# An attention and mixture kernel: every place in the order of issue chosen anew

## The chip, the core and the metric

The kernel runs on one NeuronCore of one Trainium2 chip. The core has engines that each work through a queue of their own, in the order in which the program issued to it: TensorE (matmuls, written PE in the profile, with its weight loads as PEld), VectorE (DVE), ScalarE (ACT), GpSimd (POOL) and SyncE (SP), which here issues all DMA transfers. Engines wait for one another through semaphores. SBUF is the working memory, PSUM the memory that matmuls write to, in banks of 128 partitions by 512 fp32 numbers.

The metric is the device time of one execution in microseconds (us).

## What is computed

The reference is attention with a mask, for 4 batches of 8 heads, 768 positions and 64 channels, followed by a soft mixture of 8 experts with 4 slots each. Cut to what matters:

```python
q_bits = (einsum('bhsd,dk->bhsk', q, proj) > 0)        # 6 bits per position
k_bits = (einsum('bhsd,dk->bhsk', k, proj) > 0)
mask = q_bucket[:, :, :, None] == k_bucket[:, :, None, :]   # all six bits agree
scores = where(mask, scale * q @ k.T, -1e9)
attn = exp(scores - scores.max(-1))
attn = attn / (attn.sum(-1) + 1e-9)
x = attn @ v                                   # then (batch*seq, heads*dim) = (3072, 512)

logits = x @ phi                               # 32 slots
d = softmax of logits over the 3072 rows
slot_input = d.T @ x
slot_out[e] = relu(slot_input[e] @ w1[e]) @ w2[e]
c = softmax of logits over the 32 slots
out = c @ slot_out
```

All inputs and the output are fp32.

## The kernel before

There are 32 heads (`BH`), each with six tiles of 128 positions (`NT`). Two heads form a pair, because two times 64 channels fill the 128 partitions; eight heads form a batch. The work of a head is cut into small functions, each of which issues a few instructions, often to several engines:

- `load(h)` brings q and k of a pair to the one tile `raw`. `split_hi` (ScalarE, L327) rounds them to the tile `w4`, `split_lo(h, x)` (L331, GpSimd for the first pair and VectorE for the others) takes the rest. `bits` (L365 on TensorE, L358 on VectorE) makes the bucket bits as rows. For head 0, `bits` writes the rows directly and `bits_copy` and `bits_rest` make those of head 1.
- `spread_y`, `spread_l`, `spread_x` and `spread_bits` (all L335) are DMA transfers from `w4` and the bit tile into the operands X and Y of the score matmuls; `spread_bits` is four transfers, `spread_x` two, the others one. There are three such operand tiles, used in turn. `load_v` brings v. `first_y` (POOL) fills constant rows once.
- `smax(h, t, part)` (L406) multiplies for the row maxima, into two PSUM buffers (`smx`); `most(h, n)` (L413, L416) takes the maxima on VectorE. Per head there are twelve of the one and nine of the other, since some parts share a bank. A third `smax` bank can only be written when the maximum of an earlier one has been taken.
- `shift(h)` (VectorE, L423 to L426) turns the maxima into the shift of the exponent, `shift_rows(h)` (L445, for head 0 L440) transposes it and sends it as a row into X.
- `scores(h, i, part)` (L460) multiplies the scores into three PSUM buffers (`st`), `exps(h, n)` (ScalarE, L466) takes the exponential to SBUF, again nine per head. `acc` (L474, L477) adds the exponentials on GpSimd for the row sums, and `av` (L486) multiplies them with v; the last `av` of a head ends in a copy on ScalarE (L490).
- Per pair follow `pair_sum` (L498, with a copy to the one buffer `sm`, L501), `pair_turn` (L533), `pair_rec` (three reciprocals, L505), `pair_log` (L513), `pair_add` (L525, L527) and `pair_x` (L548, L550). Per batch follow `batch_both`, `batch_max`, `batch_exp` (L660), `batch_turn` (L681, copy L683 into `sm`), `batch_scale`, `batch_slots` (L698), `batch_weigh`, `batch_share` and `batch_arrange`.
- At the end the `one_` functions do a head alone what the `pair_` functions do for two, `batch_spin` (L766, L767) transposes weights for the last product, and the experts' matmuls (L911, L962) and the output (L983) follow, which are not in the plan.

What sets the order is a plan written out as numbers. One place stands for a tile of a head, so a head has six places and a pair twelve. `at(when, f, ...)` gives each function call a place: `WHEN` holds places relative to the head's (or the pair's) first place and is used for all heads alike, once for even and once for odd heads where it has two lists; `FIRST` replaces single calls at the start and `LAST` at the end. The plan is sorted by place and issued in that order; each engine gets its queue from it. Between places the loop also frees memory pools and issues weight loads:

```python
    plan.sort(key=lambda w: w[:2])
    for slot in range(int(plan[0][0] // 1), last + 5):
...
        while plan and plan[0][0] < slot + 1:
            f, *args = plan.pop(0)[2]
            f(*args)
```

Since a place only sorts, two plans differ for an engine only where two calls that both issue to it change their order. In the plan before, each `most` has the place of its last `smax` plus 0.0005, and each `exps` that of its last `scores`, so that each follows its matmul directly.

Of the kernel before, what the change touches and what calls it, by code (L numbers as in the profile page):

```python
# [75 lines left out]

FIRST = {('load', 4): 4.476,
 ('bits', 2): 1.288,
 ('split_hi', 2): 0.833,
 ('split_lo', 2, 0): 1.029,  # L80
 ('split_lo', 2, 1): 2.366,
 ('spread_y', 2): 1.587,
 ('spread_bits', 2): 1.668,
 ('spread_l', 2): 2.667,
 ('spread_x', 2): 3.34,
 ('smax', 1, 0, 0): -1.746,
 ('smax', 1, 0, 1): -1.169,
 ('smax', 1, 1, 0): 0.452,
 ('smax', 1, 1, 1): 0.57,
 ('smax', 1, 2, 0): 1.478,  # L90
 ('smax', 1, 2, 1): 1.593,
 ('smax', 1, 3, 0): 2.035,
 ('smax', 1, 3, 1): 2.061,
 ('smax', 1, 4, 0): 2.241,
 ('smax', 1, 4, 1): 2.696,
 ('smax', 1, 5, 0): 2.774,
 ('smax', 1, 5, 1): 3.433,
 ('first_y', 1): -20.551,
 ('first_y', 2): -3.524,
 ('spread_y', 1): -14.012,  # L100
 ('spread_l', 0): -12.047,
 ('spread_bits', 1): -7.869,
 ('bits_rest',): -7.878,
 ('bits_copy',): -13.916,
 ('most', 1, 0): -1.7455,
 ('most', 1, 2): 0.4525,
 ('most', 1, 3): 0.5704999999999999,
 ('most', 1, 4): 1.4785,
 ('most', 1, 6): 2.0355000000000003,
 ('most', 1, 7): 2.0615,  # L110
 ('most', 1, 8): 2.2415000000000003,
 ('most', 1, 10): 2.7745,
 ('most', 1, 11): 3.4335}

LAST = {('one_sum', -1): 1.725,
 ('one_log', -1): 1.7251,
 ('one_turn', -1): 1.7252,
 ('one_x', -1): 1.7253,
 ('one_rec', -1): 1.7255,
 ('one_add', -1): 1.7256,  # L120
 ('one_put', -1): 3.7252,
 ('batch_max', -1): 3.7249,
 ('batch_exp', -1): 3.7253,
 ('batch_turn', -1): 3.7265,
 ('batch_scale', -1): 3.7275,
 ('batch_spin', -4, 0): 1.7254,
 ('batch_spin', -4, 1): 3.7251,
 ('batch_spin', -3, 0): 3.7252,
 ('batch_spin', -3, 1): 3.7254,
 ('batch_spin', -2, 0): 3.7256,  # L130
 ('batch_spin', -2, 1): 3.7266,
 ('one_sum', -2): -2.605,
 ('one_log', -2): -3.569,
 ('one_fold', -1): -2.008,
 ('one_turn', -2): -2.223,
 ('one_rec', -2): -1.562,
 ('one_add', -2): -1.292,
 ('one_x', -2): -0.77,
 ('one_put', -2): 0.78,
 ('acc', -1, 1): -2.422,  # L140
 ('acc', -1, 2): -2.051,
 ('acc', -1, 3): -2.05,
 ('acc', -1, 4): -0.27500000000000036,
 ('acc', -1, 5): -0.274,
 ('av', -1, 0): -2.487,
 ('av', -1, 1): -2.486,
 ('av', -1, 2): -0.9130000000000003,
 ('av', -1, 3): -0.9119999999999999,
 ('av', -1, 4): -0.13600000000000012,
 ('av', -1, 5): 0.7329999999999997}  # L150


def constants():
# [880 lines left out]
```

## Time and profile before

| | us |
|---|---|
| median of 3 runs (513.42 to 513.77) | 513.61 |
| the profiled execution | 512.31 |
| its span, from the first to the last instruction | 510.3 |

| engine | busy, share of the span | instructions |
|---|---|---|
| VectorE, row maxima L416 and L413 | 129.4 us and 65.2 us | 192 and 96 |
| ScalarE, exponentials L466 | 156.5 us | 288 |
| GpSimd, row sums L477 and L474 | 237.8 us and 58.4 us | 125 and 32 |
| TensorE, scores L460 | 175.3 us | 768 |
| TensorE, row maxima L406 | 121.6 us | 384 |
| TensorE, av L486 | 143.1 us | 768 |

The profiler's ends of matmuls are modelled and overlap, so the busy times of TensorE's lines are not what each costs; the distance between two landmarks of the same kind is. In rows of a timeline stand the start, the duration, the engine, the line, the operation, the tiles written and read, and the count of instructions merged into the row; in brackets the idle time before and who ended it. Rows of the chain in order of time have start, duration, engine, tile, line and count.

### The profile page before, as it was taken

The page shows a single profiled execution, that of the slowest core. Times are in us where ns is not written, and L with a number is a line of the kernel's source. Part 1 is how long each engine was busy: PE and PEld are TensorE (multiplying, and loading weights), DVE is VectorE, ACT ScalarE, POOL GpSimd, SP SyncE. Part 2 cuts the span into 40 slices and gives each one's busy share as a digit, 9 for nine tenths or more (in the row PEclk, how much of TensorE's full clock was granted, in tenths as well). Part 3 has the DMA queues.
Part 4 walks back from the last instruction along what each step waited for, and adds up shares of the span by engine and source line. Part 5 has one row for each costly group of instructions (what it writes and reads, how often), then busy time and mean ns, then how long its engine had stood idle before and what let it go on. Part 6 is the DMA issues. An engine that isn't in the chain of part 4 may idle for free.

```text
span 510.3 us, 8930 instructions
## 1 busy us (share of the span) xinstructions
PE 491.0 (96%) x3140; PEld 287.7 (56%) x3140; DVE 358.0 (70%) x674; ACT 242.3 (47%) x481; POOL 322.3 (63%) x200
## 2 busy tenths in 40 slices
PE   6999999999999999999999999999999999989992
PEld 4555656565655556565655565656555565544562
DVE  5685877777877788777778787878766875464133
ACT  4135545544545545454564545555455454542132
POOL 8037777768676977768587876776759786800000
PEclk9789999999999999999999999999999999999997
DMA  5765666657675767666766576766456276797987
GB/s 139 197 141 147 193 171 197 171 181 176 199 165 166 176 195 173 199 172 187 181 186 166 147 208 163 207 167 196 110 137 154 70 161 223 265 395 295 412 320 299
DMA packets 39728, 99.57 MB, mean 195 GB/s; under 512 B 7298, under 2 KB 13700, under 8 KB 39684
## 3 DMA queue, kind: packets, MB, share of 16 engines
q1 hardware_dynamic: 39684, 99.00, 67.2%
q8 instruction: 25, 0.41, 0.3%
q14 instruction: 19, 0.16, 0.1%
HBM read 52.76 MB, written 6.29 MB: 116 GB/s over the span
## 4 chain that ended last, share of the span: by engine, by line
PE 83%; DVE 9%; DMA 3%; ACT 2%; issue 1%; SPq 0%; DVEq 0%; ACTq 0%
PE st L460 24%; PE av L486 22%; PE smx L406 14%; DVE mx L416 3%; PE qs L962 3%; PE qh L911 3%; PE mi L365 2%; DVE mx L413 2%; PE mi L498 2%; PE mi L513 2%; PE mi L548 2%; PE mi L445 2%; DMA w<-w 1%; PE av L290 1%; PE mi L698 1%; DMA XY<-w 1%
## 5 line engine op out<-in xcount | busy, mean ns | idle before, releaser
L477 POOL TENSOR_TENSOR acc<-acc,pt 128x768 f32<-128x768 f32 x125 | 237.8, 1902 | 65.0 <-ACT pt L466 51.2
L466 ACT ACTIVATE pt<-st 128x512 f32<-128x512 f32 x288 | 156.5, 596 | 58.3 <-PE st L460 54.5
L460 PE MATMUL st<-XY 128*128 128x256 f32 (+1 forms) x768 | 175.3, 342 | 0.8 <-ACT pt L466 0.3
L416 DVE TENSOR_REDUCE mx<-smx 128x1 f32<-128x512 f32 x192 | 129.4, 681 | 48.7 <-PE smx L406 48.0
L486 PE MATMUL av<-pt,v 128*64 128x384 f32 x768 | 143.1, 500 | 0.0
L460 PEld LDWEIGHTS st<-XY 128*128 128x128 f32 x768 | 123.2, 190 | 19.6 <-ACT pt L466 5.1
L406 PE MATMUL smx<-XY 96*128 96x512 f32 (+1 forms) x384 | 121.6, 371 | 5.1 <-DVE mx L416 3.8
L406 PEld LDWEIGHTS smx<-XY 96*128 96x128 f32 x384 | 65.7, 191 | 54.5 <-issue 15.2
L486 PEld LDWEIGHTS av<-pt,v 128*64 128x64 f32 x768 | 48.2, 137 | 65.5 <-issue 55.4
L474 POOL TENSOR_TENSOR acc<-pt 128x768 f32<-128x768 f32 x32 | 58.4, 1825 | 34.9 <-ACT pt L466 34.7
L413 DVE TENSOR_REDUCE mx<-smx 128x2 f32<-128x512 f32 x96 | 65.2, 679 | 15.0 <-PE smx L406 14.4
L490 ACT COPY avs<-av 128x384 f32<-128x384 f32 x32 | 15.3, 477 | 61.1 <-PE av L486 61.1
L331 DVE TENSOR_TENSOR w<-raw,w 128x768 fp32r<-128x768 f32 x30 | 37.8, 1259 | 1.0 <-ACT w L327 1.0
L505 DVE RECIPROCAL sm<-sm 128x128 f32<-128x128 f32 x45 | 38.3, 907 | 0.0
L448 ACT CAST mr<-mi 12x128 fp32r<-12x128 f32 x31 | 7.9, 254 | 64.0 <-PE mi L445 53.3
L327 ACT CAST w<-raw 128x768 fp32r<-128x768 f32 x32 | 25.1, 831 | 12.6 <-DMA XY<-w 6.9
L358 DVE TENSOR_SCALAR bt<-mi,con 128x384 fp32r<-128x384 f32 x15 | 10.1, 676 | 18.2 <-PE mi L365 11.7
L550 DVE TENSOR_TENSOR xq<-mi,r 128x256 f32<-128x256 f32 x45 | 17.4, 414 | 2.1 <-PE mi L548 1.2
L445 PEld LDWEIGHTS mi<-ident,mz 128*72 128x72 f32 x31 | 3.5, 114 | 21.6 <-DVE mz L426 12.8
L365 PE MATMUL mi<-raw,pb 128*32 128x384 f32 x128 | 15.1, 517 | 0.1
L548 PE MATMUL mi<-ident,avs 128*128 128x128 f32 x90 | 14.8, 272 | 0.0
L962 PE MATMUL qs<-w 128*32 128x256 f32 x232 | 14.6, 380 | 0.0
(171 smaller groups left out, 318.0 us busy)
## 6 DMA issues: line engine op xcount, KB each, us to landing
w<-w SPq DMA_DIRECT2D x61, 512.0 KB
XY<-w SPq DMA_DIRECT2D x63, 384.0 KB
raw<-qk SPq DMA_DIRECT2D x32, 384.0 KB
XY<-w SPq DMA_DIRECT2D x64, 192.0 KB
v<-vt SPq DMA_DIRECT2D x32, 192.0 KB
out<-w SPq DMA_DIRECT2D x12, 512.0 KB
xq<-w SPq DMA_DIRECT2D x3, 512.0 KB
XY<-bt SPq DMA_DIRECT2D x62, 19.5 KB
```

What stands on the lines that cost most here:

```text
L331: (nc.vector if h else nc.gpsimd).tensor_tensor(out=w[:, 2 * x + 1], in0=st[h]["raw"][:, x], in1=w[:, 2 * x], op=ALU.subtract)
L365: nc.tensor.matmul(pts_b[j // 2 if h == 0 else 0][32 * j:32 * j + 32, 0:HC], pb[:, 32 * (j // 2):32 * (j // 2) + 32], st[h]["raw"][:, j // ...
L406: nc.tensor.matmul(pt[:, o:o + b - a], s["Y"][0:96, 0, t * P:(t + 1) * P], s["Y"][0:96, 1, a:b], start=True, stop=True)
L413: nc.vector.tensor_reduce(out=mx[:, n - 1:n + 1], in_=s["sm_ps", n - 1].rearrange("p (a x) -> p a x", a=2), axis=AX.X, op=ALU.max)
L416: nc.vector.reduce_max(out=mx[:, n:n + 1], in_=s["sm_ps", n], axis=AX.X)
L460: nc.tensor.matmul(pt[:, o:o + b - a], x[:, 1, i * P:(i + 1) * P], x[:, 0, a:b], start=first, stop=not first)
L466: nc.scalar.activation(s["P", n // 4][:, 512 * u:512 * u + 512], s["st_ps", n - (n % 4 == 2)], AF.Exp, scale=D ** -0.5)
L474: nc.gpsimd.tensor_tensor(out=s["acc"], in0=pr[:, 0:S], in1=pr[:, S:2 * S], op=ALU.add)
L477: eng.tensor_tensor(out=s["acc"], in0=s["acc"], in1=pr[:, a * S:(a + 1) * S], op=ALU.add)
L486: nc.tensor.matmul(s["av"][64 * c:64 * c + 64, 0:HC], s["v"][:, i, :], pr[:, o + c * HC:o + (c + 1) * HC], start=(i == 0), stop=(i == NT - 1))
L505: nc.vector.reciprocal(out=rs[:, k * P:(k + 1) * P], in_=rs[:, k * P:(k + 1) * P])
L962: nc.tensor.matmul(po[32 * j:32 * j + 32], hTs[g][:, f, 32 * j:32 * j + 32], wt[1, x, 2 * g + f // 4, j][:, (f % 4) * HM:(f % 4 + 1) * HM] ...
```

## The change

All numbers of `WHEN`, `FIRST` and `LAST` are replaced, and calls whose place lies after the end of the loop are issued after it. The places of `most` and `exps` are now free numbers: a maximum or an exponential can stand later in its engine's queue than directly behind its matmul. The two `av` of a tile pair, which stood 0.001 apart, have places of their own too. No function changes, so that every instruction is issued as before, in another order.

Cut to the parts with most of the calls:

```diff
-WHEN = {'load': -23.228,
- 'bits': -14.718,
- 'split_hi': -14.15,
- 'split_lo': [-13.173, -12.657],
- 'spread': [[-13.185, -11.633, -9.493, -7.304], [-10.44, -10.41, -11.057, -10.018]],
- 'load_v': [-3.955, -4.754],
...
- 'shift': [-2.803, -2.153],
- 'shift_rows': [-2.18, -2.143],
- 'av': [[3.488, 3.489, 6.789, 6.79, 7.032, 7.033], [3.202, 3.203, 4.62, 4.621, 6.466, 6.4670000000000005]],
- 'pair_sum': 15.98,
- 'pair_rec': [18.062, 18.408, 18.445],
- 'pair_log': 18.701,
- 'pair_add': 19.165,
- 'batch_exp': 22.194,
- 'batch_turn': 23.394,
- 'batch_slots': 24.562,
- 'load_weights': 4.18,
- 'most': [[-7.7205, -7.1035, -6.7585, -6.1825, -5.5425, -5.9395, -4.4195, -3.9885, -3.4575], [-7.8065, -7.7095, -7.1565, -7.0925, -4.5085, -5.3165, -2.7865, -3.8375, -5.7855]],
+WHEN = {'load': -22.0508,
+ 'bits': -14.467,
+ 'split_hi': -14.3621,
+ 'split_lo': [-13.3303, -12.2413],
+ 'spread': [[-11.312, -10.3184, -8.8177, -6.6655], [-12.6618, -9.5428, -9.5016, -10.4378]],
+ 'load_v': [-3.4958, -2.5158],
...
+ 'shift': [-2.9192, -2.4824],
+ 'shift_rows': [-2.406, -2.3767],
+ 'av': [[3.3475, 3.579, 6.7431, 6.9618, 7.1119, 7.1448], [3.0065, 3.033, 4.3979, 4.45, 6.3731, 6.7119]],
+ 'pair_sum': 15.6351,
+ 'pair_rec': [19.6428, 18.3203, 19.2569],
+ 'pair_log': 18.6723,
+ 'pair_add': 19.6831,
+ 'batch_exp': 21.1538,
+ 'batch_turn': 23.5591,
+ 'batch_slots': 27.233,
+ 'load_weights': 0.3156,
+ 'most': [[-8.0236, -7.5536, -7.3039, -6.8101, -3.9785, -5.9175, -3.4914, -3.5661, -3.1213], [-7.7877, -7.733, -6.7829, -6.5887, -3.7858, -4.368, -2.779, -2.8697, -5.5832]],
...
 FIRST = {
- ('bits', 2): 1.288,
- ('split_lo', 2, 0): 1.029,
- ('split_lo', 2, 1): 2.366,
- ('smax', 1, 1, 1): 0.57,
- ('smax', 1, 5, 0): 2.774,
- ('first_y', 1): -20.551,
- ('bits_rest',): -7.878,
- ('most', 1, 0): -1.7455,
- ('most', 1, 11): 3.4335}
+ ('bits', 2): -2.2897,
+ ('split_lo', 2, 0): 0.9772,
+ ('split_lo', 2, 1): 3.8714,
+ ('smax', 1, 1, 1): -1.1303,
+ ('smax', 1, 5, 0): 0.8476,
+ ('first_y', 1): -12.2411,
+ ('bits_rest',): -6.6255,
+ ('most', 1, 0): -1.4777,
+ ('most', 1, 11): 2.0627}
...
 LAST = {
- ('batch_exp', -1): 3.7253,
- ('batch_turn', -1): 3.7265,
- ('batch_spin', -3, 1): 3.7254,
- ('batch_spin', -2, 0): 3.7256,
- ('av', -1, 4): -0.13600000000000012,
- ('av', -1, 5): 0.7329999999999997}
+ ('batch_exp', -1): 3.5124,
+ ('batch_turn', -1): 11.6976,
+ ('batch_spin', -3, 1): 7.8316,
+ ('batch_spin', -2, 0): 1.1026,
+ ('av', -1, 4): -0.6437,
+ ('av', -1, 5): -0.0667}
...
         while plan and plan[0][0] < slot + 1:
             f, *args = plan.pop(0)[2]
             f(*args)
+    for _, _, (f, *args) in plan:
+        f(*args)
```

In order, the lists of `spread` are `spread_y`, `spread_bits`, `spread_l`, `spread_x`, for an even and for an odd head; those of `most` go by n = 0, 2, 3, 4, 6, 7, 8, 10, 11.

More of the change, by code (lines that the diff above doesn't have):

```diff
@@ L77 @@
-FIRST = {('load', 4): 4.476,
- ('bits', 2): 1.288,
- ('split_hi', 2): 0.833,
- ('split_lo', 2, 0): 1.029,
- ('split_lo', 2, 1): 2.366,
[L82 to L88, printed above, removed]
- ('smax', 1, 1, 1): 0.57,
[L90 to L95, printed above, removed]
- ('smax', 1, 5, 0): 2.774,
- ('smax', 1, 5, 1): 3.433,
- ('first_y', 1): -20.551,
[L99 to L102, printed above, removed]
- ('bits_rest',): -7.878,
- ('bits_copy',): -13.916,
- ('most', 1, 0): -1.7455,
[L106 to L112, printed above, removed]
- ('most', 1, 11): 3.4335}
@@ L115 @@
[L115 to L122, printed above, removed]
- ('batch_exp', -1): 3.7253,
- ('batch_turn', -1): 3.7265,
[L125 to L128, printed above, removed]
- ('batch_spin', -3, 1): 3.7254,
- ('batch_spin', -2, 0): 3.7256,
[L131 to L148, printed above, removed]
- ('av', -1, 4): -0.13600000000000012,
- ('av', -1, 5): 0.7329999999999997}
+WHEN = {'load': -22.0508,
[4 more added lines that the diff above has]
+ 'load_v': [-3.4958, -2.5158],
+ 'smax': [[-8.0957, -7.6074, -7.5986, -7.3951, -6.8835, -6.5658, -6.1918, -6.7371, -3.8274, -4.4389, -4.1075, -3.2098], [-8.213, -8.1654, -7.9984, -7.4588, -6.5997, -4.224, -4.1907, -5.1205, -3.11, -3.8329, -3.5375, -5.7851]],
+ 'scores': [[-0.5718, -0.7611, -0.7237, 1.0865, 1.904, 2.7786, 2.8245, 4.6954, 4.4477, 4.15, 4.199, 5.1191], [0.1895, 0.1729, 0.2241, 2.0398, 1.376, 1.3481, 2.2038, 2.6485, 4.0097, 3.7509, 3.7642, 3.6922]],
+ 'shift': [-2.9192, -2.4824],
+ 'shift_rows': [-2.406, -2.3767],
+ 'acc': [[2.9776, 5.97, 6.0776, 6.3947, 7.8217], [3.2452, 3.3311, 3.5788, 7.1015, 8.1963]],
+ 'av': [[3.3475, 3.579, 6.7431, 6.9618, 7.1119, 7.1448], [3.0065, 3.033, 4.3979, 4.45, 6.3731, 6.7119]],
+ 'pair_sum': 15.6351,
+ 'pair_turn': 17.1901,
+ 'pair_rec': [19.6428, 18.3203, 19.2569],
+ 'pair_log': 18.6723,
+ 'pair_x': [22.2866, 23.8697],
+ 'pair_add': 19.6831,
+ 'batch_both': 20.2555,
+ 'batch_max': 20.53,
+ 'batch_exp': 21.1538,
+ 'batch_turn': 23.5591,
+ 'batch_scale': 27.1824,
+ 'batch_slots': 27.233,
+ 'batch_weigh': 26.7635,
+ 'batch_share': 27.8565,
+ 'batch_arrange': 35.4675,
+ 'load_weights': 0.3156,
+ 'most': [[-8.0236, -7.5536, -7.3039, -6.8101, -3.9785, -5.9175, -3.4914, -3.5661, -3.1213], [-7.7877, -7.733, -6.7829, -6.5887, -3.7858, -4.368, -2.779, -2.8697, -5.5832]],
+ 'exps': [[-0.3703, 0.6173, 1.6874, 3.4628, 3.6275, 5.93, 5.8943, 4.8757, 6.2678], [0.5762, 0.9545, 2.3858, 2.3653, 2.6268, 3.3117, 4.8524, 4.7744, 4.4102]]}
@@ new lines @@
+FIRST = {('load', 4): 4.2929,
+ ('bits', 2): -2.2897,
+ ('split_hi', 2): 0.1962,
+ ('split_lo', 2, 0): 0.9772,
+ ('split_lo', 2, 1): 3.8714,
+ ('spread_y', 2): 2.8501,
+ ('spread_bits', 2): 2.6181,
+ ('spread_l', 2): 2.9663,
+ ('spread_x', 2): 4.9529,
+ ('smax', 1, 0, 0): -2.1381,
+ ('smax', 1, 0, 1): -2.1276,
+ ('smax', 1, 1, 0): -1.2708,
+ ('smax', 1, 1, 1): -1.1303,
+ ('smax', 1, 2, 0): -0.3195,
+ ('smax', 1, 2, 1): -0.3188,
+ ('smax', 1, 3, 0): -0.229,
+ ('smax', 1, 3, 1): -0.0509,
+ ('smax', 1, 4, 0): 0.2949,
+ ('smax', 1, 4, 1): 0.8313,
+ ('smax', 1, 5, 0): 0.8476,
+ ('smax', 1, 5, 1): 1.2089,
+ ('first_y', 1): -12.2411,
+ ('first_y', 2): -3.9607,
+ ('spread_y', 1): -11.7167,
+ ('spread_l', 0): -10.4559,
+ ('spread_bits', 1): -4.6786,
+ ('bits_rest',): -6.6255,
+ ('bits_copy',): -7.3862,
+ ('most', 1, 0): -1.4777,
+ ('most', 1, 2): -1.1735,
+ ('most', 1, 3): -0.8648,
+ ('most', 1, 4): -0.3072,
+ ('most', 1, 6): 0.1061,
+ ('most', 1, 7): 0.2652,
+ ('most', 1, 8): 0.8741,
+ ('most', 1, 10): 1.3563,
+ ('most', 1, 11): 2.0627}
@@ new lines @@
+LAST = {('one_sum', -1): 0.4395,
+ ('one_log', -1): 0.473,
+ ('one_turn', -1): 0.9482,
+ ('one_x', -1): 0.9972,
+ ('one_rec', -1): 2.5486,
+ ('one_add', -1): 2.8225,
+ ('one_put', -1): 3.8641,
+ ('batch_max', -1): 3.0906,
+ ('batch_exp', -1): 3.5124,
+ ('batch_turn', -1): 11.6976,
+ ('batch_scale', -1): 29.4023,
+ ('batch_spin', -4, 0): 14.095,
+ ('batch_spin', -4, 1): 2.5653,
+ ('batch_spin', -3, 0): 2.8407,
+ ('batch_spin', -3, 1): 7.8316,
+ ('batch_spin', -2, 0): 1.1026,
+ ('batch_spin', -2, 1): 28.251,
+ ('one_sum', -2): -3.0114,
+ ('one_log', -2): -3.4478,
+ ('one_fold', -1): -3.3092,
+ ('one_turn', -2): -2.3657,
+ ('one_rec', -2): -2.1699,
+ ('one_add', -2): -0.728,
+ ('one_x', -2): -0.5672,
+ ('one_put', -2): 0.55,
+ ('acc', -1, 1): -3.6071,
+ ('acc', -1, 2): -2.457,
+ ('acc', -1, 3): -2.2016,
+ ('acc', -1, 4): -0.1773,
+ ('acc', -1, 5): 8.4957,
+ ('av', -1, 0): -2.7175,
+ ('av', -1, 1): -2.4049,
+ ('av', -1, 2): -1.1879,
+ ('av', -1, 3): -1.0497,
+ ('av', -1, 4): -0.6437,
+ ('av', -1, 5): -0.0667}
```

12 lines of the change are left out of this document (removed).

## The prediction

> **What bounds the kernel now.** I read the page first: busy times, the chain that ended last, then the chain in order of time, and last the timelines of the first 34 us and of the last 20 us of the attention part.
>
> ```profile
> span 510.3 us, 8930 instructions
> PE 491.0 (96%) x3140; PEld 287.7 (56%) x3140; DVE 358.0 (70%) x674; ACT 242.3 (47%) x481; POOL 322.3 (63%) x200
> PE 83%; DVE 9%; DMA 3%; ACT 2%; issue 1%; SPq 0%; DVEq 0%; ACTq 0%
> ```
>
> TensorE is busy for 96% of the span and holds 83% of the chain; no other engine is near its limit. What an order of issue can gain is therefore where TensorE waits. The page's `x3140` are matmuls; waits shorter than a matmul's own tail don't show as idle time, so I don't look for gaps but follow one landmark through the chain in order of time: `pair_sum` (L498), once per pair of heads.
>
> ```profile
> 84.04 0.78 PE mi L498 x8
> ...
> 110.07 0.78 PE mi L498 x8
> ...
> 136.10 0.78 PE mi L498 x8
> ...
> 164.44 0.83 PE mi L498 x8
> ...
> 350.08 0.78 PE mi L498 x8
> ...
> 361.62 5.20 DMA XY<-w
> ...
> 379.68 0.83 PE mi L498 x8
> ```
>
> An ordinary pair takes 110.07 - 84.04 = 26.03 us and again 136.10 - 110.07 = 26.03 us. The pair that ends a batch of eight heads takes 164.44 - 136.10 = 28.34 us, because it has the batch's slot matmuls as well. The last such pair takes 379.68 - 350.08 = 29.60 us, with a 5.20 us DMA on the chain. So the middle repeats to 10 ns and loses about 29.60 - 28.34 = 1.3 us at one place. The rest of the loss is at the two ends.
>
> **The start.** TensorE first, then VectorE:
>
> ```profile
> 8.96 0.70 PE L406 MATMUL smx<-XY 96*128 96x512 f32 x3 [0.53 <-POOL w L331]
> ...
> 19.03 1.56 PE L440 MATMUL mi<-ident,mz 128*1 128x128 f32 x8
> ...
> 28.12 1.09 PE L406 MATMUL smx<-XY 96*128 96x512 f32 x2 [0.98 <-DVE mx L416]
> ...
> 30.43 2.83 PE L486 MATMUL av<-pt,v 128*64 128x384 f32 x8
> 33.18 0.43 PE L445 MATMUL mi<-ident,mz 128*72 128x128 f32 x1
> ```
> ```profile
> 9.41 1.53 DVE L358 TENSOR_SCALAR bt<-pt,con 128x384 fp32r<-128x384 f32 x1 [0.60 <-ACT pt L381]
> 10.97 0.69 DVE L416 TENSOR_REDUCE mx<-smx 128x1 f32<-128x512 f32 x1
> ...
> 16.01 0.69 DVE L416 TENSOR_REDUCE mx<-smx 128x1 f32<-128x512 f32 x1 [0.89 <-PE smx L406]
> ...
> 17.58 0.69 DVE L416 TENSOR_REDUCE mx<-smx 128x1 f32<-128x512 f32 x1 [0.29 <-PE smx L406]
> ...
> 22.37 0.42 DVE L442 CAST XY<-st 1x256 fp32r<-1x256 f32 x1 [0.18 <-PE st L440]
> ...
> 25.92 0.96 DVE L331 TENSOR_TENSOR w<-raw,w 128x768 fp32r<-128x768 f32 x1 [0.65 <-ACT w L327]
> 26.80 0.67 DVE L358 TENSOR_SCALAR bt<-mi,con 128x384 fp32r<-128x384 f32 x1
> ...
> 29.86 0.95 DVE L331 TENSOR_TENSOR w<-raw,w 128x768 fp32r<-128x768 f32 x1
> ```
>
> Until the first `shift` the chain runs through VectorE: nine row maxima (L413, L416) must end before the shift of head 0 can be transposed (L440 at 19.03). From L440 to the transpose of head 1's shift (L445 at 33.18) it is VectorE again, with nine maxima, a bit comparison (L358) and two subtractions (L331).
>
> **The change, part by part.** No instruction is added or removed; places in the queues move.
>
> *Head 0.* `bits_rest` (L358 at 9.41, 1.53 us) stands ahead of the first row maximum now and behind the fourth afterwards. The first three score matmuls are done at 8.96 + 0.70 = 9.66, so the maxima can begin 10.97 - 9.66 = 1.31 us sooner. The 1.53 us is then paid in the middle of the nine, where VectorE stood idle for 0.89 + 0.29 = 1.18 us waiting for refilled buffers. If it covers none of that idle time the step costs 1.53 - 1.31 = 0.22 us; if it covers all, it gains 0.96 us; if the comparison also shrinks to the 0.67 us of the row at 26.80, 0.86 us more. I take 0.8 (bounds -0.2 and +1.8). Behind it, the bit rows of head 1 reach SP later, but `spread_x(0)` goes ahead of them, and nothing reads them before head 1's score matmuls. On POOL `first_y(1)` moves behind the two subtractions it stood ahead of; these wait for ScalarE anyway.
>
> *Head 1.* `bits(2)` moves on TensorE from among head 0's scores to the place right behind L440, where TensorE waits for the copies of the shift rows anyway; its comparison becomes VectorE's first work after the copy at 22.37. The second subtraction, `split_lo(2, 1)`, moves behind `shift(1)`. The vector queue between 22.79 and the shift thus loses one L331 of 0.95 us and the 0.65 us that the first one stood waiting for ScalarE: 1.6 us. Against this, head 1's fourth score matmul now stands ahead of head 0's scores on TensorE and must wait for the first maximum, and those scores wait behind it, with their exponentials and `split_hi(2)` behind them. That can eat all of it (0), or the av block at 30.43 can shift into faster clock (below) and double it (3.2). I take 1.6.
>
> *The ordinary pair.* Six blocks of column-tiled matmuls (L486 with its neighbours L365, L498, L513) stand in each pair before and six after, as I count them in the two plans. POOL's accumulations keep their order. SP's transfers keep their set and change places:
>
> ```profile
> 196.81 4.17 SPq L335 DMA_DIRECT2D XY<-bt  x4
> 201.09 1.43 SPq L335 DMA_DIRECT2D XY<-w  x2
> ```
> ```profile
> 205.71 0.52 PE L406 MATMUL smx<-XY 96*128 96x512 f32 x2
> ```
>
> `spread_x` of the odd head (1.43 us of SP) goes ahead of the four bit transfers and the one-transfer `spread_l` behind them, so the last bit rows are issued at 200.98 + 1.43 - 0.7 = 201.7 instead of 196.81 + 4.17 = 200.98 (one transfer is half of 1.43); their reader starts at 205.71, so 4 us remain. I cost the ordinary pair at nothing, with 0.15 us either way per pair, some 2 us over 14.
>
> *The ends of batches.* `split_hi` overwrites the tile that the spreads read:
>
> ```profile
> 206.12 1.57 ACT L327 CAST w<-raw 128x768 fp32r<-128x768 f32 x2 [0.61 <-DMA XY<-w]
> ```
> ```profile
> 366.99 1.57 ACT L327 CAST w<-raw 128x768 fp32r<-128x768 f32 x2 [2.31 <-DMA XY<-w]
> ```
>
> ScalarE waits 0.61 us for `spread_x` in an ordinary pair, and 2.31 us in the slow one, where its exponentials, queued behind, hold TensorE. Afterwards the last reader is the single transfer of `spread_l`, and `spread_x` leaves four transfers sooner. `batch_turn` also stands 2.4 places behind `batch_exp` instead of 1.2 (twelve places are a pair, so one is 26.03 / 12 = 2.2 us). I take 1.0 of the 1.3 us (0 to 2). A new closeness: `batch_slots` moves from 24.6 to 27.2, 0.4 places ahead of the next `pair_sum`, which reuses the one `sm` buffer that it reads; two av and a transpose stand between them on TensorE, so I cost it at nothing.
>
> *The tail.*
>
> ```profile
> 447.79 1.51 PE L486 MATMUL av<-pt,v 128*64 128x384 f32 x8
> ...
> 449.71 0.87 PE L486 MATMUL av<-pt,v 128*64 128x384 f32 x4
> ...
> 450.87 0.87 PE L486 MATMUL av<-pt,v 128*64 128x384 f32 x4
> ```
> ```profile
> 458.32 0.83 ACT L767 CAST ct<-smx 128x384 fp32r<-128x384 f32 x2
> 459.05 0.30 ACT L717 ACTIVATE e<-run_n,l 64x1 f32<-64x1 f32 x1
> 459.25 0.46 ACT L683 COPY sm<-mi 128x384 f32<-128x384 f32 x1
> ```
>
> The plan has one av block fewer: two blocks of four cost 0.87 + 0.87 where one of eight costs 1.51, so 0.23 us. On ScalarE two `ct` casts (0.83 us) stand ahead of the copy that the last batch waits for; afterwards one does: up to 0.41 us. I take 0.6 (0 to 1).
>
> Sum: 0.8 + 1.6 + 0 + 1.0 + 0.6 = 4.0 us. The profiled execution has a span of 510.3 us and took 512.31 us; it should become 508.3. The median of the runs shown is 513.61, 1.30 us above it; with the same step the forecast is **509.6 us**. From the bounds the terms reach from 0 to 8, before the ordinary pair's 2 us either way.
>
> **The clock.**
>
> ```profile
> 20.00:30.00 10.00, 8.83 (x60) 5.87 (x57) 7.17 (x12) 4.57 (x8) 1.81 (x1) 0.99 0.60 141
> 30.00:34.00 4.00, 4.00 (x13) 1.69 (x14) 2.52 (x6) 0.25 (x1) 0.00 (x0) 0.57 0.47 103
> ```
>
> In 30 to 34 us TensorE's granted clock (third number from the end) was 0.57, and the av block at 30.43 took 2.83 us against 1.51 for the same eight at 447.79. Before it TensorE had waited 0.98 us at 28.12; in no part of 20 to 30 us did it stand for long (8.83 us of 10 busy). The new order makes head 1's stretch more of a trickle on TensorE, seven score matmuls in a row, each paced by a 0.69 us maximum; it can be throttled again, or not at all. [...]
>
> **The rivals.**
>
> 1. *The forecast*, 507.6 to 511.6: chance 0.52. For it: the start is bound by VectorE, where the counts above are direct.
>
> 2. *The start's gain goes back to a half clock.* At half clock the av block alone loses 2.83 - 1.51 = 1.3 us once more; two such blocks 2.6. Time: 509.6 + 1.3 to 2.6, about 511.6 to 512.9. It decides if head 1's trickle spans what throttles. Chance 0.14.
>
> 3. *A new wait in every pair: slower.* The maximum `most(h, 6)` of an even head moves behind the three reciprocals and both operations of `pair_add`:
>
> ```profile
> 195.93 2.56 DVE L505 RECIPROCAL sm<-sm 128x128 f32<-128x128 f32 x3
> ...
> 199.53 0.55 DVE L527 TENSOR_TENSOR lacc<-lacc,mi 128x384 f32<-128x384 f32 x1
> ```
> ```profile
> 197.14 2.80 PE L486 MATMUL av<-pt,v 128*64 128x384 f32 x16
> ...
> 200.33 1.34 PE L460 MATMUL st<-XY 128*128 128x256 f32 x6
> ```
>
> So it begins at 199.53 + 0.55 = 200.1 and, at 0.69 us, ends at 200.8. The matmul that needs its buffer comes after the av block, two other row-score matmuls and the six L460 that now end at 200.33 + 1.34 = 201.67. The margin is 0.9 us. If VectorE comes 0.4 us later than this margin allows, each of 14 pairs pays 0.4: 509.6 + 5.6 = 515.2. The point from which it decides is thus a delay of 0.9 us on VectorE. Against it: VectorE has 30% of its time free. Chance 0.13.
>
> 4. *More than forecast.* No half clock in the start (1.3 us more) and 0.1 us per pair: 509.6 - 1.3 - 1.4 = 506.9. Chance 0.13.
>
> 5. *The places change nothing that matters*, since engines reach the same waits in nearly the same order: 513.6. Chance 0.08.
>
> **How the numbers follow.** The range runs from 506.3, under rival 4, to 513.9, over rivals 2 and 5; outside lie rival 3 and a little of 4 and 5, under 0.2 in all. About 0.2% (1.0 us) is what a measurement of this kernel can tell from no change, so faster means below 512.6 and slower above 514.6. Faster: 0.52 + 0.13 + 0.10 of rival 2 = 0.75; same: the rest of rival 2 and rival 5, 0.12; slower 0.13.
>
> **What would show it.** Right: the first L440 near 18.2 instead of 19.03; L445 of head 1 near 30.8 instead of 33.18; ordinary periods of L498 still 26.03; no ScalarE wait of 2 us before L327; the last batch's L683 earlier relative to the last av. Wrong: ordinary periods over 26.2, with VectorE named before L406 or ScalarE before L460; another stretch at half clock after 22 us; or L445 of head 1 not earlier.

## The result, and the profile after

The changed kernel takes 509.29 us (median of 4 runs, 508.32 to 509.75) against 513.69 (513.42 to 514.83) for the kernel before on the same chip: a ratio of 0.9908 on record, interval 0.9886 to 0.9929 (the quotient of the two medians is 0.9914). The forecast was 509.6. The profiled execution took 509.0 us with a span of 507.0, so 3.3 us of span have gone.

The page of the changed kernel: span, engines, and the engines' shares of the chain that ended last.

```profile
span 507.0 us, 8943 instructions
...
PE 486.5 (96%) x3140; PEld 287.3 (57%) x3140; DVE 361.8 (71%) x674; ACT 246.9 (49%) x481; POOL 321.8 (63%) x200
...
PE 83%; DVE 6%; DMA 4%; SPq 4%; issue 1%; ACT 0%; DVEq 0%; ACTq 0%
```

TensorE is still busy for 96% of the span. VectorE's share of the chain fell from 9% to 6%, but SP's queue, which held nothing before, now holds 4%. So one wait was traded for another in part. The landmark of the prediction, the chain in order of time (start, duration, engine, tile, line, count):

```profile
56.25 0.78 PE mi L498 x8
...
82.08 0.78 PE mi L498 x8
...
107.88 0.78 PE mi L498 x8
...
119.96 3.77 DMA XY<-w
...
134.60 0.78 PE mi L498 x8
...
162.92 0.78 PE mi L498 x8
...
348.76 0.78 PE mi L498 x8
376.75 0.78 PE mi L498 x8
```

The first two pairs take 25.83 and 25.80 us (an ordinary pair took 26.03). The third takes 134.60 - 107.88 = 26.72, with a new DMA on the chain. The last batch end takes 376.75 - 348.76 = 27.99 where it took 29.60. The same starts of L498 in the timeline, all fifteen, give this account of the 3.3 us (the landmarks lie 0.07 us ahead of those of the chain):

| stretch | before | after | gained |
|---|---|---|---|
| first L406 to first L440 (head 0) | 10.07 | 8.10 | 1.97 |
| L440 to L445 of head 1 | 14.15 | 13.08 | 1.07 |
| L445 of head 1 to that of head 2 | 12.93 | 13.05 | -0.12 |
| L445 of head 2 to the first L498 | 11.52 | 12.92 | -1.40 |
| first to last L498 (14 pairs) | 373.66 | 372.39 | 1.27 |
| last L498 to the end | 79.01 | 78.47 | 0.54 |

(L406 itself began 0.07 us later.) The start gained 3.0 us up to head 1, and 1.5 of it was gone again before the first `pair_sum`. Of the middle's 1.27, 1.61 come from the one slow batch end; all other pairs together lost 0.34. These are of three kinds: the two other batch ends gained 0.09, the eight pairs that neither end a batch nor follow one gained 1.03, and the three that follow one lost 1.46.

The start after, TensorE and VectorE (timeline: start, duration, engine, line, operation, tiles, count, in brackets the idle time before):

```profile
9.03 0.70 PE L406 MATMUL smx<-XY 96*128 96x512 f32 x3 [0.85 <-DVE XY L358]
...
17.13 1.87 PE L440 MATMUL mi<-ident,mz 128*1 128x128 f32 x8
...
28.77 1.51 PE L486 MATMUL av<-pt,v 128*64 128x384 f32 x8
30.21 0.30 PE L445 MATMUL mi<-ident,mz 128*72 128x128 f32 x1
```
```profile
12.14 0.48 DVE L358 TENSOR_SCALAR bt<-pt,con 128x384 fp32r<-128x384 f32 x1
...
29.77 0.17 DVE L426 SCALAR_TENSOR_TENSOR mz<-mi,mz 128x6 f32<-128x6 f32 x1
29.85 1.25 DVE L331 TENSOR_TENSOR w<-raw,w 128x768 fp32r<-128x768 f32 x1
```

`bits_rest` takes 0.48 us instead of 1.53, the second subtraction starts behind the shift (its last operation is L426), and the av block takes 1.51 us instead of 2.83. In the kernel before, the shift of head 1 ended at 32.45 + 0.17 = 32.62:

```profile
32.45 0.17 DVE L426 SCALAR_TENSOR_TENSOR mz<-mi,mz 128x6 f32<-128x6 f32 x1
```

L445 came only at 33.18, behind the av block at half clock (0.50), which ran from 30.43 to 33.26. So TensorE, not VectorE, was the last link there. In the changed kernel too the shift is ready first, at 29.94, and L445 follows the av block at 30.21.

The windows of the start (third number from the end: granted clock):

```profile
20.00:30.00 10.00, 9.39 (x57) 5.80 (x54) 8.89 (x17) 4.11 (x7) 1.54 (x1) 1.00 0.59 129
30.00:34.00 4.00, 3.74 (x19) 2.64 (x17) 3.77 (x5) 2.68 (x6) 2.21 (x3) 1.00 0.66 167
```

The half clock in 30 to 34 us (0.57 before) did not return. An earlier stretch at half clock is in both kernels: 0.50 from 12.5 to 19.3 us here, 0.52 from 13 to 20 us before.

**Where the start's gain goes.** The chain between the two shifts of the next pair:

```profile
43.29 2.78 DMA XY<-w
...
46.91 0.83 ACT w L327
...
49.99 2.00 DVE w L331
```

SP issues the transfer from `w4` (`spread_l` of head 3) at 43.29, because earlier transfers, the four bit transfers last (4.02 us from 39.23 on), fill its queue. ScalarE's `split_hi` must wait until that transfer has read the tile. ScalarE after, and then before:

```profile
46.18 1.56 ACT L327 CAST w<-raw 128x768 fp32r<-128x768 f32 x2 [2.28 <-DMA XY<-w]
```
```profile
47.50 1.56 ACT L327 CAST w<-raw 128x768 fp32r<-128x768 f32 x2 [0.75 <-DMA XY<-w]
```

The wait is 1.5 us longer than before. In the chain an exponential, scores, a row-score matmul and a maximum follow `split_hi`, and only then the second subtraction at 49.99. That one takes 2 us beside a GpSimd accumulation, but it did so before as well (1.91 us at 51.41), so what was lost is the wait.

**Where the pairs after a batch lose.** The three pairs that follow a batch's end take 26.82, 27.05 and 26.84 us, not 25.8 (before: 26.42, 26.43 and 26.40). VectorE, then GpSimd, in the first of them:

```profile
180.29 0.95 DVE L331 TENSOR_TENSOR w<-raw,w 128x768 fp32r<-128x768 f32 x1
...
182.75 2.39 DVE L331 TENSOR_TENSOR w<-raw,w 128x768 fp32r<-128x768 f32 x1
```
```profile
180.96 1.58 POOL L757 TENSOR_TENSOR ct<-call,ct 128x96 fp32r<-128x96 f32 x4 [1.02 <-ACT ct L755]
182.51 4.32 POOL L477 TENSOR_TENSOR acc<-acc,pt 128x768 f32<-128x768 f32 x2
```

`batch_arrange` (L757) now stands in this pair (place 35.47 instead of 28.2). It pushes an accumulation on GpSimd to 182.51, just ahead of the second subtraction, which then takes 2.39 us (1.58 at 184.56 before, and 1.00 in e6 below, where `batch_arrange` has its old place).

### The profile page after: what moved, and what is told of

Read it like the earlier page. It is cut to its first block, busy times and chain, and to the rows that moved or that the text cites. A ratio compares the mean times of both kernels' runs of the same rounds, so it can differ in the third digit from the quotient of the medians.

```text
span 507.0 us, 8943 instructions
## 1 busy us (share of the span) xinstructions
PE 486.5 (96%) x3140; PEld 287.3 (57%) x3140; DVE 361.8 (71%) x674; ACT 246.9 (49%) x481; POOL 321.8 (63%) x200
## 4 chain that ended last, share of the span: by engine, by line
PE 83%; DVE 6%; DMA 4%; SPq 4%; issue 1%; ACT 0%; DVEq 0%; ACTq 0%
PE st L460 24%; PE av L486 23%; PE smx L406 14%; SPq L335 4%; PE qs L964 3%; PE qh L913 3%; DVE mx L416 2%; PE mi L513 2%; PE mi L498 2%; PE mi L365 2%; DMA XY<-w 2%; PE mi L548 2%; DVE w L331 2%; DMA fold<-cst 2%; PE mi L445 1%; PE mi L698 1%
## 5 line engine op out<-in xcount | busy, mean ns | idle before, releaser
L477 POOL TENSOR_TENSOR acc<-acc,pt 128x768 f32<-128x768 f32 x125 | 238.1, 1904 | 62.7 <-ACT pt L466 55.3
L466 ACT ACTIVATE pt<-st 128x512 f32<-128x512 f32 x288 | 162.1, 595 | 69.1 <-PE st L460 58.9
L460 PE MATMUL st<-XY 128*128 128x512 f32 (+1 forms) x768 | 176.8, 343 | 0.6 <-ACT pt L466 0.6
L486 PE MATMUL av<-pt,v 128*64 128x384 f32 x768 | 141.5, 497 | 0.0
L460 PEld LDWEIGHTS st<-XY 128*128 128x128 f32 x768 | 120.9, 190 | 22.0 <-issue 10.2
L406 PE MATMUL smx<-XY 96*128 96x512 f32 (+1 forms) x384 | 120.1, 367 | 7.2 <-DVE mx L416 4.6
L406 PEld LDWEIGHTS smx<-XY 96*128 96x128 f32 x384 | 68.4, 189 | 49.9 <-issue 14.7
L474 POOL TENSOR_TENSOR acc<-pt 128x768 f32<-128x768 f32 x32 | 58.4, 1824 | 39.8 <-ACT pt L466 39.6
L331 DVE TENSOR_TENSOR w<-raw,w 128x768 fp32r<-128x768 f32 x30 | 36.8, 1227 | 0.1
L448 ACT CAST mr<-mi 12x128 fp32r<-12x128 f32 x31 | 7.9, 256 | 58.5 <-issue 29.5
L327 ACT CAST w<-raw 128x768 fp32r<-128x768 f32 x32 | 25.1, 831 | 9.6 <-DMA XY<-w 6.4
L445 PEld LDWEIGHTS mi<-ident,mz 128*72 128x72 f32 x31 | 3.5, 113 | 19.2 <-DVE mz L426 12.3
```

The costliest lines, as they stand in the source:

```text
L331: (nc.vector if h else nc.gpsimd).tensor_tensor(out=w[:, 2 * x + 1], in0=st[h]["raw"][:, x], in1=w[:, 2 * x], op=ALU.subtract)
L406: nc.tensor.matmul(pt[:, o:o + b - a], s["Y"][0:96, 0, t * P:(t + 1) * P], s["Y"][0:96, 1, a:b], start=True, stop=True)
L460: nc.tensor.matmul(pt[:, o:o + b - a], x[:, 1, i * P:(i + 1) * P], x[:, 0, a:b], start=first, stop=not first)
L466: nc.scalar.activation(s["P", n // 4][:, 512 * u:512 * u + 512], s["st_ps", n - (n % 4 == 2)], AF.Exp, scale=D ** -0.5)
L474: nc.gpsimd.tensor_tensor(out=s["acc"], in0=pr[:, 0:S], in1=pr[:, S:2 * S], op=ALU.add)
L477: eng.tensor_tensor(out=s["acc"], in0=s["acc"], in1=pr[:, a * S:(a + 1) * S], op=ALU.add)
```

## The experiments

All start from the changed kernel; each diff shows only what differs from it (minus: changed kernel, plus: experiment). Ratios are against the kernel before, run on the same chip in the same series; kernels compared directly are of one series unless the text says otherwise.

### e1: the transfers in their old order

```diff
-WHEN = {'load': -22.0508,
+WHEN = {'load': -23.228,
- 'spread': [[-11.312, -10.3184, -8.8177, -6.6655], [-12.6618, -9.5428, -9.5016, -10.4378]],
- 'load_v': [-3.4958, -2.5158],
+ 'spread': [[-13.185, -11.633, -9.493, -7.304], [-10.44, -10.41, -11.057, -10.018]],
+ 'load_v': [-3.955, -4.754],
- 'load_weights': 0.3156,
+ 'load_weights': 4.18,
```

> The changed kernel with the places of the DMA transfers (spread, load, load_v, load_weights) as before the change. Theory: the changed kernel's ordinary pair is 25.8 to 25.9 us, 0.2 us shorter than before, but four pairs (26.7 to 27.1 us) and head 2 and 3 lose 0.8 to 1.5 us each because transfers land late in SP's new order. With the old order of transfers these pairs fall to 25.9 and the time to 505 to 507 us. Rival: the transfers land late because of the new order of everything else; then the pairs of 26.7 to 27.1 us stay and the time is 509 to 510. Second rival: the last reader of the split tile is spread_x again, ScalarE waits over 2 us for it at the ends of batches, and the time is 510 to 511.

Measured: 510.02 us, ratio 0.9946 (0.9916 to 0.9977). The late transfers of the new order looked like a plain loss, but the old order in the new plan gains nothing: the step from L445 of head 2 to the first L498 becomes 15.06 us (12.92 after, 11.52 before). The chain there has a still longer transfer:

```profile
42.90 5.62 DMA XY<-w
```

TensorE's granted clock was also 0.50 from 51.7 to 55.1 us in this trace, and an av block on the chain there takes 2.54 us instead of 1.44, so 1.1 of the 15.06 us belong to the clock. Even without them the start is no better with the old transfers alone. The 14 pairs take 371.40 us, between the 372.39 and the 370.83 of the changed kernel's two traces (e5, below), which are of other series, so no gain of the old order is shown there either. My theory, that the new transfer order costs more than it brings, fell.

### e2, e9, e10, e11: maxima and exponentials tied to their matmuls

e2 puts each `most` and `exps` 0.00005 behind its last matmul again, with TensorE's order as changed. e9 does so for the maxima alone, e10 for the exponentials alone. e11 is e2 but for one place, the maximum n = 3 of the odd heads from head 3 on (15 instructions), which stays where the change put it.

```diff
 # e2, the lists (FIRST's maxima of head 1 likewise)
- 'most': [[-8.0236, -7.5536, -7.3039, -6.8101, -3.9785, -5.9175, -3.4914, -3.5661, -3.1213], [-7.7877, -7.733, -6.7829, -6.5887, -3.7858, -4.368, -2.779, -2.8697, -5.5832]],
- 'exps': [[-0.3703, 0.6173, 1.6874, 3.4628, 3.6275, 5.93, 5.8943, 4.8757, 6.2678], [0.5762, 0.9545, 2.3858, 2.3653, 2.6268, 3.3117, 4.8524, 4.7744, 4.4102]]}
+ 'most': [[-8.09565, -7.59855, -7.39505, -6.88345, -6.19175, -6.73705, -3.82735, -4.10745, -3.20975], [-8.21295, -7.99835, -7.45875, -6.59965, -4.19065, -5.12045, -3.10995, -3.53745, -5.78505]],
+ 'exps': [[-0.57175, -0.72365, 1.08655, 1.90405, 2.82455, 4.69545, 4.44775, 4.19905, 5.11915], [0.18955, 0.22415, 2.03985, 1.37605, 2.20385, 2.64855, 4.00975, 3.76425, 3.69225]]}
 # e11: as e2, with the third number of the odd list of 'most' kept, -6.7829
```

> The changed kernel with every row maximum and every exponential put directly behind its matmul again, all other places as changed; TensorE's order is the same. Theory: the free places of the maxima and exponentials matter little, since VectorE and ScalarE have 29% and 51% of their time free: 509 to 510.5 us, ordinary pairs of 25.8 to 26.0. Rival: they are what shortens the ordinary pair, so it goes back to 26.05 or more and the time to 512 or more.

> The changed kernel with the row maxima alone put back directly behind their matmuls; the exponentials keep their free places. Theory: the maxima carry the loss of the run with both tied, since on VectorE the maximum of an odd head's n = 3 then stands ahead of the first subtraction (L331) and holds it until TensorE has done two av: 530 to 537 us. Rival: the exponentials carry it: 509 to 513.

> The changed kernel with the exponentials alone put back directly behind their matmuls. Theory: 508.5 to 511, ScalarE has half its time free. Rival: they carry the loss: 525 us or more.

> As the run with maxima and exponentials tied, but the maximum n = 3 of odd heads keeps its changed place, behind the first subtraction. Theory: this one place (15 instructions) carries most of the loss: 509 to 516 us, subtractions (L331) back to 0.95 us for the first. Rival: the loss is spread over many places: 525 us or more.

| | us | ratio (interval) | 14 pairs |
|---|---|---|---|
| e2, all tied | 535.97 | 1.0459 (1.0423 to 1.0495) | 398.50 |
| e9, maxima tied | 536.27 | 1.0467 (1.0424 to 1.0511) | 398.26 |
| e10, exponentials tied | 512.13 | 0.9977 (0.9948 to 1.0005) | 373.05 |
| e11, all tied but one place | 511.51 | 0.9967 (0.9945 to 0.9988) | 375.21 |

(e2 is of another series, on another chip, than the other three.) The new order of TensorE with tied maxima is 4.6% slower than the kernel before. It is not the many small freedoms that matter: one place gives back nearly all of it. What this place alone would cost, tied among maxima that are free, was not run. In the timeline of e2, VectorE, GpSimd and TensorE:

```profile
105.18 0.69 DVE L416 TENSOR_REDUCE mx<-smx 128x1 f32<-128x512 f32 x1 [1.00 <-PE smx L406]
105.79 1.78 DVE L331 TENSOR_TENSOR w<-raw,w 128x768 fp32r<-128x768 f32 x1
...
108.09 1.97 DVE L331 TENSOR_TENSOR w<-raw,w 128x768 fp32r<-128x768 f32 x1
```
```profile
104.91 4.33 POOL L477 TENSOR_TENSOR acc<-acc,pt 128x768 f32<-128x768 f32 x2 [1.67 <-ACT pt L466]
```
```profile
111.05 0.50 PE L406 MATMUL smx<-XY 96*128 96x256 f32 x2 [1.85 <-DVE mx L416]
```

The changed kernel in the same pair, VectorE and GpSimd:

```profile
99.46 0.95 DVE L331 TENSOR_TENSOR w<-raw,w 128x768 fp32r<-128x768 f32 x1
100.60 1.40 DVE L416 TENSOR_REDUCE mx<-smx 128x1 f32<-128x512 f32 x2 [0.19 <-PE smx L406]
101.92 1.31 DVE L331 TENSOR_TENSOR w<-raw,w 128x768 fp32r<-128x768 f32 x1
```
```profile
95.36 3.75 POOL L477 TENSOR_TENSOR acc<-acc,pt 128x768 f32<-128x768 f32 x2
100.58 4.35 POOL L477 TENSOR_TENSOR acc<-acc,pt 128x768 f32<-128x768 f32 x2 [1.47 <-ACT pt L466]
```

Tied, the maximum stands ahead of `split_lo(·, 0)` in VectorE's queue. Its matmul comes only after an av block, so VectorE stands 1.00 us behind it, and the subtraction that could have run there starts at 105.79. By then GpSimd has begun its accumulation (104.91), and both subtractions take 1.78 and 1.97 us instead of 0.95 and 1.31. All that stands behind them is late, and TensorE waits 1.85 us for a maximum. e2 has three stretches of 3.4 us at a granted clock of about 0.50 as well (from 81.3, 112.1 and 255.4 us); they can hold, estimated as half of each, at most 3 * 1.7 = 5.1 of its 26 us (the av block at 113.53 takes 2.45 us in the second, against 1.51 at 106.71). Freed, the subtraction goes first, in GpSimd's pause between 95.36 + 3.75 = 99.11 and 100.58, while the matmul is still to come. In places of the odd head, the next pair's subtraction stood at -13.173 + 6 = -7.173 before, and the matmul with its tied maximum at -7.157, behind it: no harm. The change moves the matmul up to -7.459, ahead of the subtraction (-13.330 + 6 = -7.330), and leaves the maximum at -6.783, behind it. So, of the maxima's places, it is this free one that makes TensorE's new order pay.

e10 and e11 also show what the exponentials do. With them tied, the pairs that end a batch take 29.48, 29.51 and 29.49 us (e10), against 27.97 each in the changed kernel run again (e5, below, another series on the same chip), while e10's pairs after a batch take 25.8, without the loss of 1.0 us. The free exponentials are therefore worth 1.5 us at each batch end and give 1.0 of it back in the pair behind; over the 14 pairs it is 373.05 - 370.83 = 2.2 us. (The 1.0 us is lost only while `batch_arrange` stands in that pair: e6, with the exponentials free, has 25.8 in two of the three.)

### e4, e8: the head 1 part undone

```diff
 # e4
- ('bits', 2): -2.2897,
- ('split_lo', 2, 1): 3.8714,
+ ('bits', 2): 1.288,
+ ('split_lo', 2, 1): 2.366,
 # e8
- ('split_lo', 2, 1): 3.8714,
+ ('split_lo', 2, 1): 2.366,
```

> The changed kernel with the bits of head 2 back among head 0's scores and the second subtraction back ahead of the shift of head 1. Theory: head 1's L445 goes from 30.2 to between 31.3 and 31.8 us and the time to 510.3 to 510.9. Rival: later transfers set when the pairs begin, so the first pair_sum (56.2 us) moves by under 0.4 us and the time stays at 509.3 to 509.7.

> The changed kernel with the second subtraction of head 2 back ahead of the shift of head 1. Theory: head 1's L445 goes from 30.2 to 31.1 to 31.6 us, first pair_sum and time up by 0.7 to 1.3 us. Rival: the wait for the transfers of heads 2 and 3 absorbs it, the time moves by under 0.4 us; or the earlier subtraction lets spread_x of head 2 leave sooner and the first pair_sum comes earlier.

Measured: e4 515.06 us, ratio 1.0037 (1.0013 to 1.0060); e8 510.72, ratio 0.9970 (0.9954 to 0.9986). e8 has the plainer message. VectorE, and GpSimd beside it:

```profile
30.03 1.86 DVE L331 TENSOR_TENSOR w<-raw,w 128x768 fp32r<-128x768 f32 x1
31.82 0.16 DVE L423 TENSOR_REDUCE mi<-mx 128x6 f32<-128x12 f32 x1
```
```profile
29.26 1.82 POOL L474 TENSOR_TENSOR acc<-pt 128x768 f32<-128x768 f32 x1 [11.75 <-ACT pt L466]
```

With the subtraction ahead of the shift, the step from L440 to L445 of head 1 is 14.83 us, and 13.02 in the changed kernel run beside it (e5): 1.8 us, with a median 510.72 - 508.81 = 1.9 us later. The intervals of the two ratios do not touch. So in the new order this one move is worth 1.8 us; the subtraction costs 1.86 us there, not 0.95, because GpSimd is at work. It is not the gain over the kernel before: there the same subtraction took 0.95 us, and L445 came behind the av block.

In e4 the shift comes at 31.24, but the next head loses far more. TensorE, and SP's queue:

```profile
36.43 0.77 PE L406 MATMUL smx<-XY 96*128 96x512 f32 x1 [4.89 <-DMA XY<-w]
```
```profile
28.70 3.33 SPq L335 DMA_DIRECT2D XY<-bt  x4
32.13 1.42 SPq L335 DMA_DIRECT2D XY<-w  x2
```

The bits now come late, but `spread_bits(2)` kept its changed place ahead of `spread_y(2)`, so the queue of SP stood behind them and the operand of the next matmul came 4.89 us late. e4 therefore measures the moved bits against SP's new order and not alone; it says nothing on what the bits' place is worth by itself.

### e5, e6, e7: the changed kernel again, batch_arrange back, bits_rest first

```diff
 # e5: no difference
 # e6
- 'batch_arrange': 35.4675,
+ 'batch_arrange': 28.2,
 # e7
- ('bits_rest',): -6.6255,
- ('bits_copy',): -7.3862,
+ ('bits_rest',): -8.2,
+ ('bits_copy',): -13.9,
```

> The changed kernel itself, beside the three others of this group, for a comparison on one chip. Both theories: 0.988 to 0.993 of the kernel before.

> The changed kernel with batch_arrange back at 28.2 instead of 35.4675. Theory: in the pair after a batch's end GpSimd's L757 of batch_arrange now pushes an accumulation (L477) over the start of VectorE's second subtraction (L331), which then waits for it (2.4 to 2.6 us instead of 1.0) and holds the row maxima behind it; without that the pairs of 26.8, 27.05 and 26.8 us after a batch fall to 25.9 to 26.2 and the time is 2 to 3 us below that of the changed kernel. Rival: these pairs are long because ScalarE's copies of batch_arrange are in them, which then only move to another pair: the time stays within 0.7 us.

> The changed kernel with bits_rest ahead of the first row maximum and bits_copy in its old place, as before the change. Theory: the first L440 goes from 17.1 back to 18.4 to 19.0 us and the comparison from 0.48 us back to about 1.5, beside GpSimd's subtraction; the time is 1.2 to 1.9 us above that of the changed kernel. Rival: the transfers of heads 2 and 3 set when the pairs begin, so the first pair_sum (56.2 us) moves by under 0.5 us, and so does the time.

| | us | ratio (interval) |
|---|---|---|
| e5, changed kernel | 508.81 | 0.9928 (0.9905 to 0.9950) |
| e6, batch_arrange back | 507.27 | 0.9903 (0.9883 to 0.9922) |
| e7, bits_rest first | 510.34 | 0.9946 (0.9926 to 0.9967) |

e6: the second subtraction in the first pair after a batch, with GpSimd:

```profile
182.51 1.00 DVE L331 TENSOR_TENSOR w<-raw,w 128x768 fp32r<-128x768 f32 x1
```
```profile
180.71 4.50 POOL L477 TENSOR_TENSOR acc<-acc,pt 128x768 f32<-128x768 f32 x2 [1.00 <-ACT pt L466]
```

1.00 us instead of 2.39, at nearly the same time. The pairs after a batch take 25.82, 26.58 and 25.85 us instead of 26.8 in e5, and the 14 pairs 369.21 instead of 370.83. The mechanism is shown in its place; the pairs differ by 1.6 us and the medians by 1.5, though the intervals of the ratios overlap.

e3 moved `bits_rest` alone, ahead of the `bits_copy` that writes what it reads, and has no time; e7 moves both.

e7: the step from the first L406 to L440 is 10.34 us, and 9.19 in e5. Its `bits_rest`:

```profile
8.93 2.10 DVE L358 TENSOR_SCALAR bt<-pt,con 128x384 fp32r<-128x384 f32 x1 [0.60 <-ACT pt L381]
```

In e5 it took 1.58 us at 12.47, and in the first run of the changed kernel 0.48 at 12.14. In the seven traces that have this start unchanged (after, e4, e5, e6, e8, e10, e12), `bits_rest` takes 0.48 to 2.01 us, and the step takes 7.6 us plus just this time, 8.10 to 9.63 in all. The rest of the step is 10.34 - 2.10 = 8.24 in e7 and 10.07 - 1.53 = 8.54 in the kernel before. So the place itself is worth 0.6 us against e7 and 0.9 against the kernel before, and how long `bits_rest` takes changes from run to run. A part of the 0.6 can be the clock's, which is at 0.50 from 10.7 us on in e7 and from 13.7 on in e5. The intervals of e5 and e7 overlap.

### e12: two repairs

```diff
- 'batch_arrange': 35.4675,
+ 'batch_arrange': 28.2,
- ('most', 1, 11): 2.0627}
+ ('most', 1, 11): 2.0627,
+ ('spread_l', 3): 5.35}
```

> The changed kernel with batch_arrange at 28.2, as in the run that was faster, and spread_l of head 3 moved from behind the four bit transfers to right behind spread_y. Theory: split_hi of head 4 no longer waits 2.3 us for that transfer, so the way from head 2's L445 to the first pair_sum falls from 12.9 to between 11.6 and 12.4 us: 506 to 507 us, 0.5 to 1.3 below the run with batch_arrange alone. Rival: the bit rows of head 3 come 0.7 us later and TensorE waits for them instead: no gain or 0.7 us more.

The first repair is that of e6. The second moves one transfer of head 3 in SP's queue, so that the tile which `split_hi(4)` overwrites is read earlier. Measured: 506.18 us (506.02 to 506.40), ratio 0.9877 (0.9859 to 0.9895), faster than both kernels: against e5, in another series on the same chip, the intervals of the ratios do not touch. ScalarE (L328 is L327 of the other kernels):

```profile
45.73 1.57 ACT L328 CAST w<-raw 128x768 fp32r<-128x768 f32 x2 [0.43 <-DMA XY<-bt]
```

ScalarE waits 0.43 us there instead of 2.28, and the step from L445 of head 2 to the first L498 is 56.54 - 44.67 = 11.87 us instead of 12.92. The 14 pairs take 368.04 us, with 25.8 in all three pairs after a batch. Against e6, which has the first repair alone, the step was 12.81 us; the intervals of the two ratios overlap, so the second repair is shown by its wait and its step, not by the time.

## Why the prediction was right, and where it was not

- **Sum.** Of the forecast's 4.0 us of span 3.3 came. Its terms were right in sign at both ends and in the slow batch end, but the start paid back 1.5 us behind head 2 and the pairs after a batch lost 1.5, which no term held. That 509.3 came so near to 509.6 is in part luck: a short `bits_rest` in this run (1.05) and the 1.0 us of the ordinary pairs, neither in the sum, made up for most of it.
- **Head 0** (forecast 0.8; bounds -0.2 to 1.8): 1.9 came, as L440 stands at 17.13 instead of 19.03. The mechanism is that of the step: 8.54 - 7.62 = 0.92 us of it is the comparison's new place, where it covers the idle time of VectorE (0.96 if it covers all, by the prediction). The other 1.05 is the shrinking comparison (1.53 to 0.48), left out of the sum, and luck of the run: it ends 0.2 us behind a memset on GpSimd (1.37 us from 11.03 on) that is running beside it, and in the six other traces with this start it took 0.67 to 2.01 us. This memset is that of `first_y(1)`, whose move the prediction set at nothing. In e5 the stretch took 9.19, a gain of 0.9 on the 10.07 before.
- **Head 1** (1.6): 1.07 in the stretch. The reading "it is VectorE again" was wrong in its last link: the shift was done at 32.62, and L445 waited for the av block at half clock until 33.2. At full clock that block is 1.3 us shorter (1.51 instead of 2.83), and L445 would have come right behind the shift, near 32.7; by this estimate about 0.5 of the 1.07 us is the clock's return, and no run separates the two. In the new order the second subtraction's place counts as the prediction says, with 1.8 us in e8. What the moved bits cost or gain alone stays open, because in e4 SP's queue stopped behind them.
- **Ordinary pair** (0): the eight pairs that neither end nor follow a batch take 207.36 us instead of 208.39, 0.13 less for each and within the 0.15 allowed. One step of it failed: "their reader starts at 205.71, so 4 us remain". I took the margin from one pair and measured from the issue of the bits, not from the landing of the last transfer in the queue, nor did I follow the queue through the first pairs, where it is fullest. The chain of the pair at 107.88 now runs through SP to a transfer of 3.77 us, and at 43.29 through one of 2.78; both are the `spread_l` that stands behind the four bit transfers. That wait gave 26.72 us for this pair, but only in this trace: in e5 the same pair takes 25.84. At the start it gave the 1.4 us between L445 of head 2 and the first L498, which comes back in e5 (13.12 us) and e6 (12.81); e12, which moves this one transfer, gets 11.87 there. So the sign "no ScalarE wait of 2 us before L327" failed here, with 2.28 us, where the prediction had expected the single transfer of `spread_l` to shorten it.
- **Batch ends** (1.0 of 1.3): 1.6 came at the slow one. The reason given was the shorter wait of `split_hi` and the later `batch_turn`. The wait has gone (L327 at 363.33 follows without idle time, where it had waited 2.31 us), but it has gone in e10 too (L327 at 367.25), and there, with only the exponentials tied, all three batch ends take 29.5. So the gain needs the free places of the exponentials as well, which the prediction had not priced at all. Nor had it priced the move of `batch_arrange`: its L757 on GpSimd comes into the next pair, which three times takes 1.0 us longer than a clean pair and 0.4 to 0.6 longer than before the change; e6 takes 1.6 us less over the 14 pairs.
- **Tail** (0.6): 0.54. The part for av is as worked out: the blocks now take 2.16 + 0.87 = 3.03 instead of 0.87 + 0.87 + 1.51 = 3.25. The copy L683 did leave 0.3 us earlier after the last av than before (455.66 - 448.48 = 7.18 us against 459.25 - 451.74 = 7.51), but this came to nothing. The changed kernel's last av on TensorE, the copy on ScalarE, and VectorE, which shows what was late next:

```profile
447.61 0.87 PE L486 MATMUL av<-pt,v 128*64 128x384 f32 x4
```
```profile
455.66 0.48 ACT L683 COPY sm<-mi 128x384 f32<-128x384 f32 x1
```
```profile
458.14 0.28 DVE L729 TENSOR_SCALAR fold<-fold,li 128x128 f32<-128x128 f32 x1 [1.00 <-DMA fold<-cst]
458.34 0.86 DVE L703 SCALAR_TENSOR_TENSOR run_x<-run_x,al,st 128x256 f32<-128x256 f32 x2
```

L703, which the last matmuls need, stands behind L729, and that one waits 1.00 us for a transfer (0.59 before). From the last av to the end it is 58.5 us in both kernels, so all of the 0.54 lies ahead of it; what made up the part beyond the av blocks' 0.22 was not followed.
- **The rivals.** The half clock (2) did not come back: TensorE's granted clock is 1.00 from 20 to 34 us; why it stayed up is not shown. The new wait in each pair (3) isn't there in the clean pairs, which are shorter. The case "more than forecast" (4) met both of its conditions, the full clock and 0.1 us per ordinary pair, but the shift allowed less than the 1.3 us of the clock, and the gain was paid back behind head 2 and in the pairs after a batch.
- **What I had not seen**: that one free place among the maxima is the condition of the rest. The prediction weighed `most(h, 6)` of the even head, a place with 0.9 us to spare, and not `most(h, 3)` of the odd one. With all maxima tied the changed kernel is 4.6% slower than the kernel before (e2); freeing that place alone takes it back to a ratio of 0.9967 (e11).

## What to carry to other kernels

When a matmul is moved up, ask what stands behind the instruction that consumes it, on the consumer's engine: a consumer that is issued at once and waits also holds everything behind it, and here one place in 9 was worth about 25 us (ratio 1.0459 in e2 to 0.9967 in e11). Count for each moved call what it does on every queue, GpSimd and SP included, in the pair into which it moves, not only where it left. And margins of a queue are taken at the place where it is fullest, from the landing of the last transfer.
